# Linear attention and channel mix on one core: fused passes for the first batch, and another written-out order

## The chip, the cores and the metric

The kernel runs on one core of one Trainium2 chip. The metric is the device time of one execution in microseconds (us). The core has five engines with an instruction queue each: TensorE (PE, the matrix products), VectorE (DVE), ScalarE (ACT), GpSimd (POOL, which here mostly issues loads) and SyncE (SP, which issues stores and small copies). An engine takes its queue in order; an instruction that waits holds up all that stand behind it. Transfers are made by 16 DMA engines, whichever queue issued them.

## What is computed

Eight batches b, eight heads, 576 tokens s, 64 dimensions per head; F = 1024. All inputs and the output are fp32, the kernel computes in bf16 with fp32 sums.

```python
kv  = einsum('bhsd,bhse->bhde', k, v)
u   = einsum('bhsd,bhde->bhse', q, kv)
x   = u / sqrt(mean(u*u, -1) + 1e-6) * g_norm        # per head; then heads side by side: 512 channels
xp  = x one token later, zero in front
xk  = mu_k*x + (1-mu_k)*xp ;  xr = mu_r*x + (1-mu_r)*xp
out = sigmoid(xr @ w_r) * (relu(xk @ w_k)**2 @ w_v)
```

## The kernel before

The work is cut into named *pieces*, each a handful of instructions for one engine. A string, ORDER, lists all pieces by name, and `Plan.emit` issues them in that order; so every engine's queue has its pieces in the order of that one list. A name may end in `@A` or `@D`, which puts the piece on ACT or DVE. `z:512` is a matmul on zeros that computes nothing and stands where PE would have no work.

**Attention, batch b.** Channels are held in two halves z = 0, 1 (four heads each). Batches 0 and 1 go half by half, with names such as `kv0.1` (batch 0, z = 1); from batch 2 on both halves go together (`kv4.01`). The pieces of one batch, in the order in which each needs the one before:

- `ld.k`, `ld.v`, `ld.q` load from HBM, on POOL (L221, L226), with a cast to bf16. The first half of k and v of batch 0 comes over SP as fp32 (`ldh`, L236) and is cast by `cst`. `ld.wk`, `ld.wv`, `ld.wr` load the weights (L252). Each of k, v and q has three buffers, so a load for a later batch waits until a buffer is free. POOL also waits, at each load, for the load eight places before it.
- `kv` (PE, L265) makes the 64 x 64 products, `kc` copies them out of PSUM, `ks` (PE, L271) sorts even and odd rows apart, `kd` copies again. `tq` (DVE, L349) transposes q.
- `u` (PE, L282) gives u, 128 channels x 288 tokens at a time for each of two channel blocks, transposed, into a PSUM tile `ps`. There are four such tiles in all.
- `uc` multiplies u by g_norm and writes it to SBUF as `uT` (DVE L136 or ACT L134). `sq` (ACT, L370) writes the squares; `ss` (PE, L395 in batches 0 and 1, L379 later) sums them over each head's 64 channels; `rs` (ACT, L288) makes 1/rms. From batch 2 on 1/rms is made once per head and `sp` (SP, L417) spreads it over the channels by eight small DMAs per batch.
- `mul` (DVE, L392) makes x = uT times 1/rms, into `xT`. `d` (L300) is x minus the token before. `mk` and `mr` scale d by mu - 1 (DVE L136 or ACT L134) into `md`, and `xk`, `xr` (L313) add x.

**Channel mix, group g of 512 tokens** (nine groups; group g needs the batches that its tokens lie in: group 0 batch 0, group 1 batches 0 and 1, group 2 batches 1 and 2, and so on): `k` (PE, L469 in group 0, L494 later), `relu` (ACT, L452), `ksq` (DVE, L480, L509), `v` (PE, L541), `r` (PE, L521), `sig` (ACT, L531), `out` (DVE, L554), `st` (SP, L443). In group 1 the k pieces are halved again (`k1.4.0`, `k1.4.1`).

In ORDER, mix pieces of earlier groups stand between the attention pieces of later batches, so that PE has matmuls while a batch's chain runs over DVE and ACT.

Of the kernel before, what the change touches and what calls it, by code (L numbers as in the profile page):

```python
# [10 lines left out]
ALU = mybir.AluOpType  # L11
# [1 line left out]


ORDER = """
ldh.k ldh.v ld.q0.0 small table seta setp ident ld.v0.1 ld.k0.1 ld.q0.1 ld.q1.0 ld.v1.0 ld.k1.0 perm ld.wk0 ld.wk1 ld.k1.1 ld.v1.1 ld.wv0 ld.q1.1 ld.wv1 ld.wr ld.k2.01 ld.v2.01 ld.q2.01 zz cst.k0@A cst.k1@A cst.v1@D cst.v0@A z:512 z:512 z:512 z:512 z:512 z:512 z:512 z:512 z:512 z:512 z:512 z:512 z:512 z:512 z:512 z:512 kv0.0 setb tq0.0.1 kc0.0@A z:512 z:512 ks0.0 tq0.0.0 tr9 kd0.0@D z:512 z:512 z:512 u0.0.1 sq0.01 kv0.1 ld.v3.01 ld.k3.01 cols u0.0.0 sq0.00 uc0.01@D uc0.00@A kc0.1@D z:512 z:512 z:512 ss0.00 rs0.00 z:512 ss0.01 tq0.1.0 tq0.1.1 ld.q3.01 mul0.00 ks0.1 kd0.1@A d0.00 rs0.01 z:512 z:512 u0.1.0 uc0.10@A sq0.10 u0.1.1 uc0.11@A z:512 z:512 z:512 z:512 z:512 ss0.10 mul0.01 d0.01 mk0.00@D kv1.0 sq0.11 xk0.00 rs0.10 ss0.11 rs0.11 tq1.0.1 kc1.0@D ks1.0 tq1.0.0 kd1.0@A z:512 z:512 u1.0.0 mk0.01@D u1.0.1 sq1.00 xk0.01 k0.100 uc1.00@A uc1.01@A k0.000 sq1.01 mul0.10 d0.10 mk0.10@D xk0.10 mul0.11 d0.11 k0.010 mr0.11@A mk0.11@D xk0.11 k0.011 relu0.01 ss1.1 rs1.1 mr0.10@D xr0.10 k0.001 k0.101 relu0.00 mr0.00@D relu0.10 kv1.1 k0.110 ss1.0 ksq0.00 ksq0.10 k0.111 kc1.1@A v0.3.0 tq1.1.0 v0.2.0 tq1.1.1 ld.q4.01 ld.k4.01 ld.v4.01 rs1.0 relu0.11 ks1.1 kd1.1@D ksq0.11 mr0.01@A xr0.11 ksq0.01 xr0.00 v0.1.0 mul1.0 d1.0 u1.1.1 uc1.11@A u1.1.0 sq1.10 sq1.11 v0.0.0 xr0.01 v0.0.1 uc1.10@A v0.1.1 ss1.3 rs1.3 ss1.2 v0.3.1 rs1.2 mk1.0@D xk1.0 r0.0 mul1.1 d1.1 r0.1 sig0.0 r0.2 r0.3 sig0.1 v0.2.1 kv2.01 ld.v5.01 ld.k5.01 mk1.1@D xk1.1 out0.0 k1.2.0 k1.0.0 k1.1.0 out0.1 kc2.01@D ks2.01 tq2.01.1 tq2.01.0 k1.3.0 k1.2.1 k1.3.1 mr1.0@A kd2.01@A relu1.1 k1.0.1 u2.01.1 sq2.11 mr1.1@D k1.1.1 relu1.0 k1.6.0 k1.7.0 uc2.01@D uc2.11@D sq2.01 ksq1.1 u2.01.0 k1.6.1 k1.7.1 sq2.10 xr1.1 uc2.10@D k1.4.0 sq2.00 k1.5.0 uc2.00@D ss2 rs2 sp2.0 kv3.01 ld.v6.01 ld.q5.01 k1.4.1 k1.5.1 xr1.0 relu1.2 r1.0 kc3.01@D ksq1.0 ks3.01 kd3.01@A relu1.3 tq3.01.1 tq3.01.0 ld.q6.01 ld.k6.01 ksq1.2 r1.1 v1.0.0 ksq1.3 u3.01.0 uc3.10@D sig1.0 sq3.10 v1.1.0 v1.0.1 tq4.01.1 v1.1.1 uc3.00@D u3.01.1 tq4.01.0 sq3.00 uc3.11@A r1.2 r1.3 out1.0 sq3.11 v1.2.0 v1.3.0 sq3.01 ss3 mul2.0 sig1.1 kv4.01 ld.k7.01 ld.q7.01 ld.v7.01 sp2.1 rs3 kc4.01@A d2.0 v1.3.1 mk2.0@D xk2.0 st0.0 ks4.01 kd4.01@A v1.2.1 st0.3 uc3.01@A st0.2 mul2.1 d2.1 mk2.1@D xk2.1 u4.01.0 sq4.10 st0.1 uc4.10@A k2.2 uc4.00@A sq4.00 out1.1 st1.0 mr2.0@D k2.3 k2.0 k2.1 relu2.0 ksq2.0 relu2.1 ksq2.1 k2.4 k2.5 relu2.2 k2.6 k2.7 sp3.0 relu2.3 xr2.0 v2.3.0 mr2.1@D kv5.01 mul3.0 ksq2.2 u4.01.1 sq4.11 ksq2.3 sp3.1 d3.0 v2.2.0 st1.1 v2.2.1 uc4.11@A v2.1.0 uc4.01@A mul3.1 sq4.01 mr3.0@D ss4 xr3.0 kc5.01@A v2.1.1 v2.3.1 rs4 sp4.1 xr2.1 sp4.0 r2.2 v2.0.0 d3.1 mk3.1@A mr3.1@D xr3.1 xk3.1 tq5.01.0 ks5.01 kd5.01@A mk3.0@D xk3.0 v2.0.1 r2.3 sig2.1 out2.1 st2.3 r2.0 tq6.01.1 r2.1 sig2.0 out2.0 k3.2 k3.3 relu3.1 ksq3.1 k3.0 tq5.01.1 k3.4 k3.5 relu3.2 k3.1 mul4.1 d4.1 mr4.1@D relu3.0 ksq3.0 k3.6 k3.7 ksq3.2 u5.01.0 st2.0 st1.3 uc5.10@D relu3.3 ksq3.3 v3.3.0 uc5.00@A xr4.1 r3.0 mul4.0 sq5.10 tq6.01.0 r3.1 sq5.00 mk4.1@D sig3.0 r3.2 d4.0 mk4.0@D xk4.0 st2.1 r3.3 sig3.1 v3.3.1 kv6.01 kc6.01@A u5.01.1 uc5.11@D uc5.01@A sq5.11 tq7.01.1 v3.2.0 v3.2.1 ks6.01 kd6.01@D out3.1 v3.0.0 v3.0.1 st2.2 sq5.01 u6.01.1 xk4.1 ss5 rs5 sp5.0 v3.1.0 v3.1.1 mr4.0@D xr4.0 uc6.11@A st1.2 sq6.11 sq6.01 uc6.01@A tq7.01.0 k4.4 k4.5 k4.2 out3.0 st3.0 u6.01.0 relu4.2 uc6.10@D uc6.00@D sq6.10 k4.3 relu4.1 sq6.00 k4.0 k4.1 relu4.0 ksq4.1 k4.6 kv7.01 ss6 st3.2 ksq4.0 k4.7 r4.0 r4.1 kc7.01@D mul5.0 d5.0 relu4.3 ksq4.3 v4.1.0 sp5.1 mul5.1 rs6 st3.1 d5.1 ks7.01 kd7.01@D sp6.1 v4.2.0 ksq4.2 v4.3.0 sig4.0 u7.01.0 uc7.10@D v4.0.0 v4.2.1 v4.0.1 mk5.0@D mr5.1@A uc7.00@A sq7.00 r4.2 sq7.10 r4.3 mk5.1@D xk5.1 xr5.1 mr5.0@A sig4.1 mul6.1 xr5.0 xk5.0 d6.1 mk6.1@A sp6.0 mul6.0 v4.3.1 v4.1.1 out4.0 out4.1 st4.0 st4.2 k5.6 k5.7 relu5.3 ksq5.3 k5.2 k5.3 relu5.1 st4.3 ksq5.1 k5.0 k5.1 relu5.0 u7.01.1 sq7.01 sq7.11 d6.0 xk6.1 mk6.0@D uc7.11@D mr6.0@D k5.4 k5.5 st3.3 ksq5.0 r5.2 xr6.0 r5.3 st4.1 mr6.1@D ss7 uc7.01@A relu5.2 rs7 v5.1.0 sig5.1 ksq5.2 r5.0 sp7.0 r5.1 sig5.0 v5.0.0 v5.0.1 v5.1.1 xk6.0 k6.0 k6.1 relu6.0 xr6.1 r6.0 sp7.1 out5.0 st5.0 st5.1 v5.3.0 mul7.1 v5.2.0 k6.4 k6.5 relu6.2 ksq6.2 d7.1 ksq6.0 k6.2 k6.3 relu6.1 r6.1 mul7.0 r6.2 sig6.0 r6.3 k6.6 k6.7 v5.2.1 ksq6.1 v6.2.0 v6.3.0 d7.0 relu6.3 v6.1.0 mr7.0@A mk7.0@D xk7.0 v6.0.0 sig6.1 mr7.1@A mk7.1@D xk7.1 k7.4 k7.5 xr7.0 ksq6.3 v6.1.1 v6.0.1 out6.0 v6.3.1 v6.2.1 out6.1 st6.3 k8.2 k8.3 relu8.1 k7.2 v5.3.1 out5.1 k7.6 k7.7 k8.0 relu7.3 k7.3 relu7.1 ksq8.1 relu7.2 st6.0 st6.1 ksq7.3 st6.2 xr7.1 k7.0 k7.1 r7.0 relu7.0 r7.2 r7.1 r7.3 k8.1 k8.6 sig7.0 ksq7.2 ksq7.0 ksq7.1 k8.7 relu8.3 st5.3 relu8.0 r8.2 r8.3 st5.2 ksq8.0 v7.3.0 ksq8.3 v7.3.1 v7.1.0 v7.1.1 sig8.1 k8.4 k8.5 relu8.2 ksq8.2 v7.0.0 v7.0.1 v7.2.0 v7.2.1 sig7.1 out7.1 st7.2 st7.3 out7.0 v8.1.00 r8.0 r8.1 v8.2.00 v8.2.10 st7.0 v8.0.00 out8.20 sig8.0 st7.1 v8.1.10 st8.20 out8.10 v8.0.10 st8.10 v8.3.00 v8.3.10 out8.00 st8.00 out8.30 v8.3.01 v8.3.11 st8.30 out8.31 st8.31
"""


# [37 lines left out]
def kernel(  # L57
# [13 lines left out]
    nc = tc.nc  # L71
# [18 lines left out]
    X0 = 2  # L90
# [203 lines left out]
    def blends(b, z, name, x0, w, deps, mds, dd):  # L294
        xT = xTs[(NZ * b + z) % NX]
        cur, prev = slice(X0 + x0, X0 + x0 + w), slice(X0 - 1 + x0, X0 - 1 + x0 + w)
        cs, r0 = slice(x0, x0 + w), S * (b % RB) + x0

        def diff(_):
            nc.vector.tensor_tensor(out=get(dd)[:, :, cs], in0=xT[:, :, cur], in1=xT[:, :, prev], op=ALU.subtract)  # L300

        df = add("d" + name, "D", diff, deps=deps, bufs=[dd, x_buf[(b, z)]])
        done = {}
        for key, dst, m0 in (("k", xk, 0), ("r", xr, NHP)):
            md = mds[key]

            def mul(eng, md=md, m0=m0):
                for y in range(2):
                    hp = m0 + 2 * z + y
                    scale(eng, get(md)[:, y, cs], dd.t[:, y, cs], cols[:, hp:hp + 1])  # L310

            def plus(_, md=md, dst=dst):
                nc.vector.tensor_tensor(out=dst[:, 2 * z:2 * z + 2, r0:r0 + w], in0=md.t[:, :, cs], in1=xT[:, :, cur],  # L313
                                        op=ALU.add)

            m = add(f"m{key}" + name, "DA", mul, deps=[df, p_cols], bufs=[dd, md])
            done[key] = add(f"x{key}" + name, "D", plus, deps=[m] + x_free.get((b - RB, key), []),
                            bufs=[md, x_buf[(b, z)]])
        return done
# [3 lines left out]
    def attention(b):  # L323
# [40 lines left out]
        for z in range(NZ):  # L364
            for i, (c0, c1) in enumerate(PARTS):
                name, ps, w, cs = f"{b}.{z}{i}", us[z][i], c1 - c0, slice(c0, c1)
                uT, sq = bufs[z]["uT"], bufs[z]["sq"]
                uc = add("uc" + name, "DA", lambda eng, ps=ps, uT=uT, cs=cs, w=w: scale(
                    eng, get(uT)[:, :, cs], ps.t[:, :, 0:w], cols[:, 8:9]), deps=[pu[(z, i)], p_cols], bufs=[ps, uT])
                sq_ = add("sq" + name, "A", lambda _, ps=ps, sq=sq, cs=cs, w=w: nc.scalar.activation(  # L370
                    out=get(sq)[:, :, cs], in_=ps.t[:, :, 0:w], func=AF.Square), deps=[pu[(z, i)]], bufs=[ps, sq])
# [15 lines left out]
        for z in range(NZ):  # L387
            uT, sq, rs, dd = (bufs[z][t] for t in ("uT", "sq", "rs", "d"))
            xT, xb = xTs[(NZ * b + z) % NX], x_buf[(b, z)]

            def mul(_, cs, uT=uT, rs=rs, xT=xT):
                nc.vector.tensor_mul(out=xT[:, :, X0 + cs.start:X0 + cs.stop], in0=uT.t[:, :, cs], in1=rs.t[:, :, cs])  # L392

# [3 lines left out]
            if b == 0:  # L397
                muls = []
                for i, (c0, c1) in enumerate(PARTS):
                    ps, w, cs = Buf("ps"), c1 - c0, slice(c0, c1)  # L400
                    s = add(f"ss{b}.{z}{i}", "T", lambda _, ps=ps, c0=c0, w=w, sq=sq: [ones_mm(_, ps, y, c0, w, y, sq)
                            for y in range(2)], deps=[secs[(z, i)][1], p_setb], bufs=[ps, sq])
                    p = add(f"rs{b}.{z}{i}", "A", lambda _, ps=ps, w=w, cs=cs, rs=rs: rms(_, get(rs)[:, :, cs], ps.t[:, :, 0:w]),
                            deps=[s], bufs=[ps, rs])
                    muls = muls + [add(f"mul{b}.{z}{i}", "D", lambda _, cs=cs, mul=mul: mul(_, cs),
                                       deps=[p, secs[(z, i)][0], p_setb], bufs=[uT, rs, xb])]
                    done = blends(b, z, f"{b}.{z}{i}", c0, w, muls, mds[z], dd)
                    for key in "kr":
                        x_ready[b][key].append(done[key])
# [200 lines left out]
```

## Time and profile before

| | |
|---|---|
| median of 3 runs | 200.04 us (199.97 to 200.71) |
| the profiled execution | 200.29 us |
| its span, first to last instruction | 198.5 us |
| PE busy | 189.4 us, 95% of the span |
| DVE busy | 136.1 us, 69% |
| ACT busy | 123.6 us, 62% |
| DMA | 30.63 MB, mean 154 GB/s |

A page of the profile gives busy time by engine, the span in 40 slices, the chain of work that ended last, and groups of like instructions by source line. Beside it the trace can be asked for the instructions of an engine in order of time: start, duration, engine, line, operation, out<-in, how many, and in brackets how long the engine sat idle before and what released it. Busy time of one engine is an average over stretches with different limits; what decides is which wait ends last in a stretch.

### The profile page before, as it was taken

Reading aid. Unit: us, or ns where it says so; the run is one execution under the profiler, and the core shown is the slowest. Engines: PE = TensorE matmul, PEld = TensorE weight load, DVE = VectorE, ACT = ScalarE, POOL = GpSimd, SP = SyncE. Lnnn points to the kernel's source line nnn. Section 1 sums busy time; section 2 is a strip of 40 time slices with the busy share of each in tenths; the row PEclk is TensorE's granted clock in tenths of the full one; section 3 lists DMA queues with packets and bytes.
Section 4 is the critical chain, followed back from the end, with each engine's and each line's share of the span. In section 5 each row is a group of like instructions: output and inputs, shape, how many; then the busy total and the mean of one; then the engine's idle time right before and its main releaser. Section 6 shows DMA issues by size and latency. Waiting matters only on the chain.

```text
span 198.5 us, 4247 instructions
## 1 busy us (share of the span) xinstructions
PE 189.4 (95%) x1741; PEld 94.1 (47%) x1765; DVE 136.1 (69%) x242; ACT 123.6 (62%) x161; POOL 23.8 (12%) x42
## 2 busy tenths in 40 slices
PE   7998999998997999999999999999999999999992
PEld 2444864443544454444547744434444444444451
DVE  1579939999899378999986679896348246410631
ACT  3378995769897776848676697689255423652120
POOL 7843332220412100000000000000000000000000
PEclk9999999999999999999999999999999999999999
DMA  6999999999999999999706523242500017000064
GB/s 218 217 207 210 193 204 212 211 207 214 207 237 273 272 239 243 217 241 262 187 0 188 147 47 77 95 169 58 170 0 2 0 45 273 2 0 0 28 239 159
DMA packets 21031, 30.63 MB, mean 154 GB/s; under 512 B 1932, under 2 KB 14484, under 8 KB 21012
## 3 DMA queue, kind: packets, MB, share of 16 engines
q0 software_dynamic: 11280, 16.19, 45.6%
q1 hardware_dynamic: 9588, 14.03, 22.4%
q8 instruction: 14, 0.23, 0.5%
q10 hardware_dynamic: 144, 0.13, 0.2%
q14 instruction: 5, 0.04, 0.1%
HBM read 33.56 MB, written 9.44 MB: 217 GB/s over the span
## 4 chain that ended last, share of the span: by engine, by line
PE 66%; DMA 27%; POOL 3%; issue 1%; DVE 0%; POOLq 0%
PE ps L541 25%; PE ps L494 25%; DMA v<-in_v_dram 13%; PE ps L521 12%; DMA k<-in_k_dram 9%; DMA w_k<-in_moe_w_k_dram 6%; PE ps L282 2%; PE ps L265 1%; POOL k L226 1%; PE ps L379 1%; POOL v L226 1%; POOL q L221 1%; POOL perm L189 1%; PE ps L271 0%; DVE out L568 0%
## 5 line engine op out<-in xcount | busy, mean ns | idle before, releaser
L541 PE MATMUL ps<-w_v,sqk 128*128 128x512 bf16 (+1 forms) x287 | 66.4, 373 | 0.9 <-issue 0.5
L494 PE MATMUL ps<-xk,w_k 128*128 128x512 bf16 (+1 forms) x280 | 58.1, 355 | 0.6 <-issue 0.3
L452 ACT ACTIVATE relu<-ps 128x1024 bf16<-128x1024 f32 x36 | 36.1, 1025 | 35.6 <-PE ps L494 33.7
L541 PEld LDWEIGHTS <-sqk 128*128 128x128 bf16 x296 | 27.8, 98 | 32.1 <-issue 2.0
L494 PEld LDWEIGHTS <-w_k 128*128 128x128 bf16 x288 | 27.5, 98 | 27.3 <-issue 1.6
L509 DVE TENSOR_TENSOR sqk<-relu 128x1024 bf16<-128x1024 bf16 x32 | 21.7, 687 | 22.8 <-ACT relu L452 22.8
L521 PE MATMUL ps<-w_r,xr 128*128 128x512 bf16 x140 | 33.5, 379 | 0.3
L554 DVE TENSOR_TENSOR out<-ps,sig 128x1024 f32<-128x1024 f32 x16 | 19.2, 1218 | 12.4 <-PE ps L541 8.5
L531 ACT ACTIVATE sig<-ps 128x1024 bf16<-128x1024 f32 x18 | 18.3, 1022 | 9.2 <-PE ps L521 9.1
L370 ACT ACTIVATE sq<-ps 128x576 bf16<-128x576 f32 x32 | 20.0, 652 | 5.7 <-PE ps L282 4.1
L521 PEld LDWEIGHTS <-xr 128*128 128x128 bf16 x144 | 14.0, 98 | 16.5 <-issue 0.2
L136 DVE TENSOR_SCALAR md<-d,cols 128x576 bf16<-128x576 bf16 (+1 forms) x54 | 16.4, 347 | 0.3
L349 DVE STREAM_TRANSPOSE qT<-q 128x576 f32<-128x576 f32 (+1 forms) x20 | 14.9, 762 | 2.3 <-DMA q<-in_q_dram 2.1
L134 ACT ACTIVATE uT<-ps,cols 128x576 bf16<-128x576 f32 x19 | 13.7, 741 | 2.0 <-PE ps L282 1.9
L392 DVE TENSOR_TENSOR xT<-uT,rs 128x1152 bf16<-128x1152 bf16 (+1 forms) x18 | 12.4, 686 | 2.4 <-DMA rs<-rsc 2.3
L134 ACT ACTIVATE md<-d,cols 128x576 bf16<-128x576 bf16 (+1 forms) x18 | 12.0, 714 | 2.7 <-DVE d L300 2.7
L136 DVE TENSOR_SCALAR uT<-ps,cols 128x576 bf16<-128x576 f32 x13 | 10.4, 813 | 4.7 <-PE ps L282 3.2
L144 ACT ACT_TABLE_LOAD x10 | 12.8, 1283 | 0.9 <-PEq L594 0.7
L313 DVE TENSOR_TENSOR xr<-md,xT 128x1152 bf16<-128x1152 bf16 (+1 forms) x18 | 12.3, 687 | 0.7 <-ACT md L134 0.6
L313 DVE TENSOR_TENSOR xk<-md,xT 128x1152 bf16<-128x1152 bf16 (+1 forms) x18 | 12.4, 691 | 0.5
L300 DVE TENSOR_TENSOR d<-xT 128x1152 bf16<-128x1152 bf16 (+1 forms) x18 | 12.4, 691 | 0.4
L437 PE MATMUL ps<-zero 128*128 128x512 bf16 x32 | 10.8, 478 | 1.7 <-DVE ident L167 1.2
(49 smaller groups left out, 110.8 us busy)
## 6 DMA issues: line engine op xcount, KB each, us to landing
out_dram<-out SPq DMA_DIRECT2D x35, 256.0 KB, 3.1
k<-in_k_dram POOLq DMA_DIRECT2D x6, 576.0 KB, 24.8
v<-in_v_dram POOLq DMA_DIRECT2D x6, 576.0 KB, 25.4
q<-in_q_dram POOLq DMA_DIRECT2D x6, 576.0 KB, 25.1
rs<-rsc SPq DMA_DIRECT2D x48, 72.0 KB, 5.4
q<-in_q_dram POOLq DMA_DIRECT2D x4, 288.0 KB, 8.8
w_k<-in_moe_w_k_dram POOLq DMA_DIRECT2D x2, 512.0 KB, 12.5
w_v<-in_moe_w_v_dram POOLq DMA_DIRECT2D x2, 512.0 KB, 16.3
```

Source lines behind the costliest of these rows:

```text
L134: nc.scalar.mul(out=dst, in_=src, mul=col)
L136: nc.vector.tensor_scalar(out=dst, in0=src, scalar1=col, scalar2=None, op0=ALU.mult)
L313: nc.vector.tensor_tensor(out=dst[:, 2 * z:2 * z + 2, r0:r0 + w], in0=md.t[:, :, cs], in1=xT[:, :, cur], op=ALU.add)
L349: nc.vector.transpose(out=dst[part, js], in_=src[part, js])
L370: sq_ = add("sq" + name, "A", lambda _, ps=ps, sq=sq, cs=cs, w=w: nc.scalar.activation(out=get(sq)[:, :, cs], in_=ps.t[:, :, 0:w], func=AF ...
L452: nc.scalar.activation(out=get(rt), in_=ps.t, func=AF.Relu)
L494: nc.tensor.matmul(get(ps)[:, fc % 2, a0:a1], w_k_sb[:, cc, 128 * fc:128 * fc + 128], xk[:, cc, x0:x0 + a1 - a0], start=(cc == 0), stop=(c ...
L509: nc.vector.tensor_mul(out=get(sqk)[:, 2 * f2:2 * f2 + 2, :], in0=rt.t, in1=rt.t)
L521: nc.tensor.matmul(get(ps)[:, ci % 2, :], xr[:, cc, n0:n0 + 128], w_r_sb[:, cc, :], start=(cc == 0), stop=(cc == NHP - 1))
L531: nc.scalar.activation(out=get(sg), in_=ps.t, func=AF.Sigmoid)
L541: nc.tensor.matmul(get(ps)[:, bank, cs], sqk.t[:, fc, 128 * ci:128 * ci + 128], w_v_sb[:, fc, cs], start=(fc == 0), stop=(fc == NFC - 1))
L554: dv = add(f"out{g}.{c2}", "D", lambda _, ps=ps, sg=sg, ot=ot: nc.vector.tensor_mul(out=get(ot), in0=ps.t, in1=sg.t), deps=ms + [sg_done], ...
```

## The change

In batch 0 only, `uc` goes. `mul` there takes u straight out of PSUM and multiplies by g_norm and by 1/rms in one DVE instruction. `mk` and `xk`, and `mr` and `xr`, become one pass on DVE per channel block, `(d * (mu-1)) + x`, two instructions of 288 tokens for a piece. u's PSUM tile is therefore held until `mul`. No other batch's instructions change.

And ORDER is another one: 33 matmuls on zeros in place of 34; `uc` and the batch 0 scalings gone; loads, attention pieces, mix pieces, their engines (`@A`, `@D`) and stores placed anew.

```diff
@@ blends
+            if b == 0:
+                def both(_, m0=m0, dst=dst):
+                    for y in range(2):
+                        hp = m0 + 2 * z + y
+                        nc.vector.scalar_tensor_tensor(out=dst[:, 2 * z + y, r0:r0 + w], in0=dd.t[:, y, cs], scalar=cols[:, hp:hp + 1],
+                                                       in1=xT[:, y, cur], op0=ALU.mult, op1=ALU.add)
+
+                done[key] = add(f"x{key}" + name, "D", both, deps=[df, p_cols], bufs=[dd, x_buf[(b, z)]])
+                continue
@@ attention
-                uc = add("uc" + name, "DA", lambda eng, ps=ps, uT=uT, cs=cs, w=w: scale(
+                uc = None if b == 0 else add("uc" + name, "DA", lambda eng, ps=ps, uT=uT, cs=cs, w=w: scale(
...
+            def mul_ps(_, cs, ps, rs=rs, xT=xT):
+                nc.vector.scalar_tensor_tensor(out=xT[:, :, X0 + cs.start:X0 + cs.stop], in0=ps.t[:, :, 0:cs.stop - cs.start],
+                                               scalar=cols[:, 8:9], in1=rs.t[:, :, cs], op0=ALU.mult, op1=ALU.mult)
...
-                    muls = muls + [add(f"mul{b}.{z}{i}", "D", lambda _, cs=cs, mul=mul: mul(_, cs),
-                                       deps=[p, secs[(z, i)][0], p_setb], bufs=[uT, rs, xb])]
+                    muls = muls + [add(f"mul{b}.{z}{i}", "D", lambda _, cs=cs, mul=mul_ps, pu_=us[z][i]: mul(_, cs, pu_),
+                                       deps=[p, pu[(z, i)], p_cols, p_setb], bufs=[us[z][i], rs, xb])]
```

Of the two orders, the loads in POOL's queue, first to last:

```
before  q0.0 v0.1 k0.1 q0.1 q1.0 v1.0 k1.0 wk0 wk1 k1.1 v1.1 wv0 q1.1 wv1 wr k2 v2 q2 v3 k3 q3 q4 k4 v4 v5 k5 v6 q5 q6 k6 k7 q7 v7
after   q0.0 q0.1 k0.1 v0.1 v1.1 wk0 k1.1 wk1 q1.1 k1.0 v1.0 q1.0 wv0 wv1 wr v2 q2 k2 q3 v3 k3 v6 v5 v4 k5 q4 k4 v7 k6 q5 q6 k7 q7
```

PE's pieces from the end of the first zeros to the first matmul of mix 0 (z: a matmul on zeros):

```
before  kv0.0 z z ks0.0 tr9 z z z u0.0.1 kv0.1 u0.0.0 z z z ss0.00 z ss0.01 ks0.1 z z u0.1.0 u0.1.1 z z z z z ss0.10 kv1.0 ss0.11 ks1.0 z z u1.0.0 u1.0.1 k0.100
after   kv0.0 tr9 ks0.0 z z u0.0.0 z z z ss0.00 u0.0.1 z z z z ss0.01 kv0.1 z z ks0.1 z z u0.1.0 u0.1.1 z z ss0.10 z z k0.000
```

PE's pieces from kv3 to kv5:

```
before  kv3.01 k1.4.1 k1.5.1 r1.0 ks3.01 r1.1 v1.0.0 u3.01.0 v1.1.0 v1.0.1 v1.1.1 u3.01.1 r1.2 r1.3 v1.2.0 v1.3.0 ss3 kv4.01 v1.3.1 ks4.01 v1.2.1 u4.01.0 k2.2 k2.3 k2.0 k2.1 k2.4 k2.5 k2.6 k2.7 v2.3.0 kv5.01
after   kv3.01 v1.1.1 ks3.01 r1.0 r1.1 u3.01.0 v1.0.1 r1.2 r1.3 u3.01.1 v1.3.0 v1.2.0 v1.2.1 ss3 v1.3.1 kv5.01 k2.0 k2.2 k2.3 k2.1 k2.6 k2.7 k2.4 k2.5 ks5.01 kv4.01
```

DVE's pieces of batch 0's half 0 and 1 after the change: `tq0.0.0 kc0.0 tq0.0.1 cols tq0.1.0 mul0.00 d0.00 tq0.1.1 mul0.01 d0.01 xk0.01 xk0.00 mul0.10 d0.10 xk0.10 mul0.11 d0.11 xk0.11`; and from mix 1's end on `out1.1 tq4.01.1 ksq2.1 ksq2.0 mul3.0 tq4.01.0 ksq2.3 kc4.01`. SP's queue: before `sp2.0 sp2.1 st0.0 st0.3 st0.2 st0.1 st1.0 sp3.0 sp3.1 st1.1 sp4.1`, after `sp2.1 sp2.0 st0.2 st0.0 st0.1 sp3.0 sp3.1 st1.0 st1.1 st0.3 sp4.0`.

## Prediction

> **What bounds the kernel now.** I read the page first, then TensorE's timeline, then the timeline of POOL (which issues the loads) with each load's time to landing, and last the chain of waits.
>
> ```profile
> span 198.5 us, 4247 instructions
> ...
> PE   7998999998997999999999999999999999999992
> ...
> DMA  6999999999999999999706523242500017000064
> ```
>
> Each digit is a tenth of a slice of 198.5/40 = 4.96 us. PE is full nearly throughout; the DMA engines are full from slice 2 to slice 19, up to 94 us. So there are two bounds at once: PE's work, and the stream of inputs. They meet where PE asks for a load. The PE timeline names the one place after 31 us where PE idles for a load:
>
> ```profile
> 49.47 0.77 PE L265 MATMUL ps<-v,k 64*64 64x64 bf16 x72
> ...
> 61.02 0.43 PE L379 MATMUL ps<-sq,heads 128*32 128x288 bf16 x8
> 62.30 0.77 PE L265 MATMUL ps<-v,k 64*64 64x64 bf16 x72 [0.85 <-DMA v<-in_v_dram]
> ```
>
> L265 is a kv piece. The one at 62.30 is kv4.01; it stood ready at 61.45 and waited 0.85 us for v4. The chain that ended last runs through the same load, and from there PE alone is on it:
>
> ```profile
> 37.22 24.95 DMA v<-in_v_dram
> 62.17 0.14 issue
> 62.30 0.77 PE ps L265 x72
> ...
> 188.62 6.08 PE ps L541 x36
> ```
>
> PE's other idle stretches after 62.3 are "issue" gaps of 0.16 us and less. So from 62.30 to PE's end at 194.72 the kernel is 132.4 us of packed PE work, and any wait of PE after that moves the end one for one.
>
> **When loads land.** POOL's issue times plus each one's time to landing, loads numbered in the order of issue: 15th (w_r) 33.9, k2 36.9, v2 39.6, 18th q2 42.4, v3 45.2, k3 48.5, 21st q3 51.4, q4 54.2, k4 57.7, 24th v4 62.2, 25th v5 67.7, 26th 72.3, 27th 76.5, 28th 79.3, 29th 82.1, 30th 86.0, 31st 89.8, 32nd 93.2, 33rd 98.8. All land in order. Undisturbed, a whole-batch load takes (51.4 - 33.9)/6 = 2.9 us. After 50 us the SP queue's transfers share the engines. In 54 to 70 us the loads moved 2.03 MB and the SP queue 2.08 MB; at 0.59 MB in 2.9 us the loads alone would have moved 3.25 MB, so the SP queue's 2.08 MB cost 1.22 MB of loads, 6.0 us, or 2.9 us per MB. One batch's eight rs<-rsc pieces (0.59 MB) then cost 1.7 us, one store (0.26 MB) 0.75 us. Check on today's 25th: 51.4 + 4 x 2.9 + 1.7 + 5 stores x 0.75 = 68.5 against 67.7 measured.
>
> The Trainium skill ("DMA: Bandwidth & Descriptors", section on queues, rings and completion order) says that each DMA engine takes turns between the queue rows that have work, packet by packet. The rows agree in kind: spacing 5.5 us from v4 to v5, nearly twice 2.9.
>
> **The change, part by part.** It has two halves, fusing in batch 0 and a new order.
>
> *Fusing.* In batch 0, four uc pieces go (one on DVE at 0.82 us, three on ACT at 0.73), and the four muls at 0.46 now read PSUM. No row shows that fused form. From below it costs what mul cost, 0.46; from above uc and mul in series, 0.82 + 0.46 = 1.28. I take 0.82: one pass over 576 fp32 out of PSUM, which is L136's row. The eight blends lose two scalings each (0.245 per half, or 0.48 on ACT) and a sum (0.46), and get two fused passes of 288. From below each is 0.245 (the scaling alone), from above 0.46 (a whole sum). I take 0.46, next start after 0.38 as in the rows of sums. Sum on DVE: before 4 x 0.46 + 0.82 + 6 scalings x 0.49 + 8 x 0.46 = 9.3; after 4 x 0.82 + 16 x 0.38 = 9.4. So DVE gains nothing; ACT gives up 3 x 0.73 + 2 x 0.96 = 4.1 us. With 0.245 per pass DVE would gain 2.2.
>
> The Trainium skill ("VectorE: DVE Perf Modes", rules for kernel authors) speaks against this half: chained Vector operations should not be fused for speed. The rows above, summed, say the same of DVE and not of ACT.
>
> *Opening, by rows.* u0.0.0 starts about 10.35 (10.19 now; kc0.0 stands behind a transpose of 0.68 on DVE). Then sq 0.65, ss 0.41, rs 0.74 with hand-overs of 0.05: mul0.00 at 12.8 (now 14.14). Then 0.82 + d 0.46 + tq0.1.1 0.70 gives 14.7; mul0.01 0.82, d 0.46, four fused passes 3 x 0.38 + 0.46: xk0.00 at 17.6. The first matmul of mix 0 comes at 17.7 instead of 19.66. But at 19.66 PE had also done kv1.0 0.69, ks1.0 0.33, u1.0 0.69 and ss0.11 0.25, together 1.96, which now come later. So the opening is worth 17.7 + 1.96 - 19.66 = 0. With the fused pass at 0.245 it is 0.5 better; with the form out of PSUM at 1.28 it is 2 x 0.46 = 0.9 worse. All of this stands ahead of the load waits below: a faster opening only makes PE wait longer there.
>
> *Loads.* The first 15 are the same ones in another order, so w_r, the last of them, lands at 33.9 as now. Then come v2, q2, k2, q3, v3, k3 (18th 42.4, 21st 51.4), and now **v6 as 22nd, then v5, v4, k5, q4, k4, v7, k6**. v6 is needed only by kv6; it takes a slot ahead of v5, v4 and k5. kv5 is also moved ahead of kv4 on PE, and all of mix 2's k pieces stand behind kv5.
>
> I now put PE's arrival at each kv, from its time before plus the pieces now ahead of it, against the load that it needs.
> - kv2 needs the 18th, 42.4. Before 40.38; now eight k1 halves (0.43) more and one v piece (0.86) less: 43.0. No wait.
> - kv3 needs the 21st, 51.4. Before 49.31; two k1 halves and two v pieces more: 51.9. No wait, without margin.
> - kv5 takes the place of kv4. PE is done with what stands ahead at 61.45 + v1.2.1 and v1.3.1 (2 x 0.86) = 63.2. It needs k5, the 25th: 51.4 + 4 x 2.9 + one rs group 1.7 + three stores 2.2 = 66.9. (v4's buffer comes free with kv3, at about 52; k5 is behind v4 in POOL's queue. Two loads are then still on their way, so the stream doesn't run dry.) **PE waits 3.7 us.** Everything behind kv5 in PE's queue waits too: k2.0 to k2.7, which need no load.
> - kv4 needs k4, the 27th: 51.4 + 6 x 2.9 + two rs groups 3.4 + about three stores 2.2 = 74.4. PE arrives at 66.9 + 0.7 + 32 matmuls x 0.216 + ks5 0.2 = 74.7. No wait to 1 us.
> - kv6 needs k6, the 29th, 82.1 by today's row; PE arrives at 74.7 + 0.7 + 7 v pieces 6.0 + ks4, u4 1.0 = 82.4. kv7 comes beyond 100 for a load at 93.2.
>
> Sum: kv5 at 67.0 against what is now 62.30 + 1.73 = 64.0, so PE's end moves 3.0 us, 194.7 to 197.7; the tail of 3.8 us is unchanged. The 0.85 of today is within this, since 64.0 counts it. The profiled execution was 200.29 us (span 198.5 and 1.8 around it); 203.3 by it. The median of the runs shown, 200.04, is 0.25 lower: **203.0**.
>
> **Bounds.** Loads at the fastest spacing (2.7, q2 behind v2) and one store fewer put k5 at 65.4, 1.5 sooner: 201.5. k4 in today's 27th slot, 76.5, puts kv4 1.8 later: 204.8. Behind kv4 a wait is added on DVE: mul3.0 waits for sp3's pieces, and tq4.01.0, ksq2.3 and kc4.01 are queued behind it, for whom ks4.01 and u4 wait on PE. ss3 is done about 63, rs3 about 64.5; four pieces take 4.0 us on SP and 5.4 to 8.3 to land: 73.9 to 76.8. The early end costs nothing, the late one about 1.5 us; I take nothing, as the median of the landings is the early end.
>
> **Rivals.**
> 1. *The loads are no later than PE* (faster). If k5 came at 51.4 + 4 x 2.7 = 62.2 and k4 at 67.6, as if rs and stores took nothing, neither kv5 nor kv4 would wait; today's 0.85 goes, and perhaps 0.5 of the opening: 198.9. It decides where k5 lands before 63.2. Against it: v4 to v5 took 5.5 us. For it: fewer stores stand ahead.
> 2. *Partly so* (no change): k5 at 64 to 64.8, stores late enough to pass behind it: 200.0 to 200.8.
> 3. *The opening fails*: DVE, which has to read PSUM later, holds four PSUM tiles longer and delays the k pieces. Since PE has 3.7 us in hand at kv5, it has to lose more than that to show. Then 205 and more, with waits for DVE ahead of 50 us.
> 4. *Loads at half pace while the SP queue has work.* From 52 to 65 us SP would be busy 13 us, which costs 6.5 in place of 3.9: k5 at 69.5, 205.6. For it: 5.5 us from v4 to v5; against it: 3.6 us each from q3 to v4, with SP busy from 50.5. This is what the skill's turn-taking makes of it if every packet counts alike.
>
> **How the numbers follow.** Forecast (wait at kv5, or split between kv5 and kv4, 201.3 to 205.0) 0.72; rival 1 0.07; rival 2 0.10; rivals 3 and 4 0.11. A measurement of this kernel can tell about 0.5% from no change, here 199.04 to 201.04. Faster 0.07, same 0.11, slower 0.82. The range leaves out rival 1, half of rival 2 and the far end of 3 and 4: 200.6 to 205.3.
>
> **What would show it.** PE's row of L265 x72 near 67 with idle before it of 2.5 to 4 us, released by DMA k. k3 landing near 51.4 and k5 at 65 to 68. The first k0 matmul at 17 to 18.5. PE packed from kv4 on. Fused passes of 0.35 to 0.46, the one out of PSUM near 0.82. I am wrong if kv5 starts by 64 without a wait, or if the order has waits for DVE or ACT above 1 us behind kv4, which I only laid out as far as kv6.

## The result, and the profile after

The changed kernel takes 207.88 us (median of 6 runs, 207.15 to 213.71), the kernel before in the same sessions 200.47 (6 runs, 199.97 to 200.75). One run of the six, 213.71, stands apart with a mean granted clock of 0.95 against 0.98 and is left out of the ratio. The ratio is 1.036, with an interval of 1.034 to 1.039. The forecast was 203.0, in 200.6 to 205.3: the direction was right, the time lies above the range, and the forecast loss was less than half of the measured one. The profiled execution took 208.0 us, with a span of 206.2 against 198.5: 7.7 us to explain.

The page of the changed kernel, the lines that answer to those shown of before, and with them the granted clock:

```profile
span 206.2 us, 4250 instructions
...
PE   7998899999994599999999999999999999999992
...
PEclk9999999999999579999999999999999999999999
DMA  6999999999999999996304425204400202601044
```

A slice is now 206.2/40 = 5.16 us; counted from 0, most of the loss is in slices 12 and 13, from 62 to 72 us, where PE is 0.4 and 0.5 busy. The granted clock falls there too, to 0.5 and 0.7 in slices 13 and 14. After 77 us both lines are full to the end, as they were before.

PE's timeline of the changed kernel over that place (L265 is a kv piece, L507 k, L554 v, L388 ss):

```profile
62.90 0.43 PE L388 MATMUL ps<-sq,heads 128*32 128x288 bf16 x8
63.26 1.04 PE L554 MATMUL ps<-w_v,sqk 128*128 128x512 bf16 x4
67.90 1.18 PE L265 MATMUL ps<-v,k 64*64 64x64 bf16 x72 [3.60 <-ACT rsc L288]
70.61 8.92 PE L507 MATMUL ps<-xk,w_k 128*128 128x512 bf16 x32 [1.53 <-DVE xk L313]
79.36 0.39 PE L271 MATMUL ps<-kvn,perm 128*128 128x128 bf16 x4
79.68 0.78 PE L265 MATMUL ps<-v,k 64*64 64x64 bf16 x72
```

The row of 67.90 is kv5. It starts 0.9 us later than the forecast said (67.0), after the idle time that it said (3.60 against 3.7), but what released it is ACT's rsc, not a load. Then there is a second wait, 1.53 us for xk, which the forecast did not have. Then mix 2's 32 k matmuls take 8.92 us, where 32 x 0.216 = 6.9 was expected. The clock explains the last. PE's windows of the changed kernel (length, PE busy and its instructions, granted clock, DMA share, GB/s):

```profile
64.00:65.00 1.00, 0.30 (x2) 1.00 1.14 247
65.00:66.00 1.00, 0.00 (x0) 1.00 1.03 228
66.00:67.00 1.00, 0.00 (x0) 1.00 1.00 236
67.00:68.00 1.00, 0.10 (x9) 0.77 1.11 270
68.00:69.00 1.00, 1.00 (x72) 0.50 1.12 277
...
73.00:74.00 1.00, 1.00 (x4) 0.50 1.18 215
74.00:75.00 1.00, 1.00 (x5) 0.82 1.18 217
```

PE falls idle at 64.30. The clock is halved at about 67.5 (0.77 is 0.54 of that window at 1.0 and the rest at 0.5) and is back at about 74.4 (0.82 is 0.36 of the window at 0.5): it is half through kv5 and the first 3.8 us of k2.

The chain of waits of the changed kernel says where xk came from (rsc is 1/rms before its spread; L430 is SP's spread of it over the partitions, L405 mul, L300 d, L136 md, L313 xk):

```profile
51.52 1.28 ACT L144
...
52.82 0.74 ACT rsc L288
...
59.07 7.78 DMA rs<-rsc
...
66.97 0.77 DVE xT L405
...
69.21 1.35 DVE xk L313 x2
70.56 0.05 issue
70.61 8.92 PE ps L507 x32
```

Read from the bottom: k2 waits for xk2, xk2 for mul2, mul2 for the last piece of batch 2's spread (SP sends eight one after the other, and the last lands at 66.85), and the spread for rs2 on ACT at 52.82, right behind its table load. Before, the same steps stood here, on ACT and then on DVE:

```profile
49.70 0.74 ACT L288 ACTIVATE rsc<-ps,eps 128x576 bf16<-128x576 f32 x1
```

```profile
61.52 0.76 DVE L392 TENSOR_TENSOR xT<-uT,rs 128x1152 bf16<-128x1152 bf16 x1
...
63.80 0.76 DVE L313 TENSOR_TENSOR xk<-md,xT 128x1152 bf16<-128x1152 bf16 x1
```

So rs2 is 3.1 us later than before and the end of xk2 6.0 us later (64.56 to 70.55). Before, xk2 was ready 0.9 us ahead of k2's start at 65.45: there was no room for it.

**The sum**, from the two profiled executions. When PE is done with what stands ahead of kv5, it is 64.30; before, the same work and no more was done at 61.45 + 1.73 = 63.18: 1.1 us are lost by then. The two idle stretches are 3.60 + 1.53, against 0.85 before: 4.3. At half clock k2 takes 8.92 in place of 7.07 and kv5 1.18 in place of 0.78 (rows at full clock: k2's from the second experiment below, a kv piece's at 79.68 above): 2.25. Together 7.65 of 7.7.

### The profile page after: what moved, and what is told of

The parts are those of the page before. It is cut to its first block, busy times and chain, and to the rows that moved or that the text cites. A ratio compares the mean times of both kernels' runs of the same rounds, so it can differ in the third digit from the quotient of the medians.

```text
span 206.2 us, 4250 instructions
## 1 busy us (share of the span) xinstructions
PE 194.0 (94%) x1764; PEld 94.9 (46%) x1764; DVE 136.4 (66%) x231; ACT 122.7 (59%) x160; POOL 23.9 (12%) x42
## 4 chain that ended last, share of the span: by engine, by line
PE 75%; DMA 10%; ACT 3%; DVE 3%; POOL 3%; SPq 2%; issue 1%; POOLq 0%; DVEq 0%; ACTq 0%
PE ps L554 27%; PE ps L507 26%; PE ps L534 13%; DMA w_k<-in_moe_w_k_dram 7%; DMA rs<-rsc 4%; PE ps L482 3%; SPq L430 2%; PE ps L282 2%; PE ps L265 2%; ACT relu L465 1%; PE ps L271 1%; ACT sq L379 1%; PE ps L388 1%; DVE xk L313 1%; ACT L144 1%
## 5 line engine op out<-in xcount | busy, mean ns | idle before, releaser
L554 PE MATMUL ps<-w_v,sqk 128*128 128x512 bf16 (+1 forms) x296 | 67.2, 374 | 0.2 <-ACT relu L465 0.2
L507 PE MATMUL ps<-xk,w_k 128*128 128x512 bf16 (+1 forms) x288 | 59.9, 363 | 1.5 <-DVE xk L313 1.5
L554 PEld LDWEIGHTS <-sqk 128*128 128x128 bf16 x296 | 27.8, 98 | 32.3 <-issue 2.6
L507 PEld LDWEIGHTS <-w_k 128*128 128x128 bf16 x288 | 28.1, 99 | 30.2 <-issue 3.4
L134 ACT ACTIVATE md<-d,cols 128x576 bf16<-128x576 bf16 x20 | 14.4, 769 | 6.5 <-DVE d L300 6.5
L405 DVE TENSOR_TENSOR xT<-uT,rs 128x1152 bf16<-128x1152 bf16 x14 | 10.4, 751 | 9.2 <-DMA rs<-rsc 9.1
L300 DVE TENSOR_TENSOR d<-xT 128x1152 bf16<-128x1152 bf16 (+1 forms) x18 | 12.4, 691 | 0.5
L136 DVE TENSOR_SCALAR uT<-ps,cols 128x576 bf16<-128x576 f32 x13 | 10.4, 811 | 3.0 <-PE ps L282 2.6
L136 DVE TENSOR_SCALAR md<-d,cols 128x576 bf16<-128x576 bf16 x36 | 11.5, 364 | 0.3
L134 ACT ACTIVATE uT<-ps,cols 128x576 bf16<-128x576 f32 x15 | 10.9, 743 | 1.0 <-PE ps L282 1.0
L265 PE MATMUL ps<-v,k 64*64 64x64 bf16 x576 | 8.1, 200 | 3.6 <-ACT rsc L288 3.6
L226 POOL DMA_DIRECT2D v<-in_v_dram x9 | 6.6, 739 | 38.8 <-PE ps L265 33.2
## 6 DMA issues: line engine op xcount, KB each, us to landing
q<-in_q_dram POOLq DMA_DIRECT2D x4, 288.0 KB, 10.2
```

The source lines that it names most:

```text
L134: nc.scalar.mul(out=dst, in_=src, mul=col)
L136: nc.vector.tensor_scalar(out=dst, in0=src, scalar1=col, scalar2=None, op0=ALU.mult)
L507: nc.tensor.matmul(get(ps)[:, fc % 2, a0:a1], w_k_sb[:, cc, 128 * fc:128 * fc + 128], xk[:, cc, x0:x0 + a1 - a0], start=(cc == 0), stop=(c ...
L554: nc.tensor.matmul(get(ps)[:, bank, cs], sqk.t[:, fc, 128 * ci:128 * ci + 128], w_v_sb[:, fc, cs], start=(fc == 0), stop=(fc == NFC - 1))
```

## The experiments

The theory that came to stand, D in the later expectations: batch 2's spread is late, and holds PE twice. rsc has a single buffer, so rs3 on ACT can't write it while the spread of batch 2 still reads it; until rs3 has read ss3's PSUM tile, none of the four PSUM tiles is free for kv5. And xk2 holds k2. PE has no other work left, since the new order has all of mix 1 behind it and k2 in front. The idle time then halves the clock. The rival from the forecast: k5's load, which lands at 67.4 here (forecast 66.9), holds kv5 and everything else follows.

**1. k5 loaded early.** In POOL's queue, k5 and v6 change places:

```diff
-... v3 k3 v6 v5 v4 k5 q4 k4 ...
+... v3 k3 k5 v5 v4 v6 q4 k4 ...
```

> The changed kernel with one swap in POOL's queue: ld.k5.01 where ld.v6.01 stands (22nd), ld.v6.01 where ld.k5.01 stands (25th). Theory A (two waits in series, and a clock that falls after them): kv5 no longer waits for k5 and starts at about 64.3, but k2.0 still waits for xk2, whose last sum ends at 70.5 because batch 2's spread of 1/rms lands at 66.9; PE stands idle 65.0 to 70.6, the clock falls as before, and the time moves by less than 0.7 us: 207.2 to 208.2. Rival B (the late load k5 is the whole of the loss): the 3.6 us wait at kv5 goes with nothing in its place, 203.5 to 204.5, or 201.5 to 202.5 if the clock then stays up too.

Median 207.45 us (207.06, 207.84, 208.19, and one run of 203.69). k5 landed at 53.7, 13.7 us sooner than in the changed kernel, and kv5 moved by one. PE's timeline:

```profile
66.91 0.77 PE L265 MATMUL ps<-v,k 64*64 64x64 bf16 x72 [2.89 <-ACT rsc L288]
69.62 0.61 PE L507 MATMUL ps<-xk,w_k 128*128 128x512 bf16 x1 [1.93 <-DVE xk L313]
```

These rows are of the run of 208.19. In it the load is not what holds kv5 by itself. The run of 203.69 has a mean granted clock of 1.00, in a span of 201.9, and lies where the rival expected it. It is one run, and no profile shows its waits. The half clock costs k2 about 2.9 us in the profiled run (69.62 to 79.58 in place of 7.07), so the kept clock could be most of the 4.5 us between the two, and the rest is open.

**2. Zeros in the idle time.** Matmuls on zeros into the tiles that kv5 and k2 then overwrite; the output is the same:

```diff
-... v1.3.1 mr2.1@A kv5.01 ... xk2.0 k2.0 ...
+... v1.3.1 mr2.1@A [16 matmuls on zeros] kv5.01 ... xk2.0 [7 matmuls on zeros] k2.0 ...
```

> The changed kernel with matmuls on zeros in PE's queue where it stood idle: 16 ahead of kv5.01 (3.5 us at full clock, into kv5's own PSUM tile) and 7 ahead of k2.0 (1.5 us, into that one's tile). They compute nothing and wait for nothing new. Theory A: the granted clock, 0.50 from 67.9 to about 74.5 in the changed kernel, stays at 1.0; kv5 still starts about 67.9 and k2.0 about 70.7, but k2's 32 matmuls take 6.9 us in place of 8.9, and the end comes 2.0 us sooner: 205.9 (205.5 to 206.3). If the slow matmuls have another cause than the idle PE (contention, the load stream), the clock stays at 0.50 and the time at 207.9 or above.

208.78 us, ratio 1.042 (1.039 to 1.045): a miss on the time, and telling. PE's timeline:

```profile
67.03 3.61 PE L599 MATMUL ps<-zero 128*128 128x512 bf16 x16 [2.43 <-ACT rsc L288]
70.57 0.90 PE L265 MATMUL ps<-v,k 64*64 64x64 bf16 x72
...
72.92 7.07 PE L511 MATMUL ps<-xk,w_k 128*128 128x512 bf16 x32
```

The zeros need no load and no data, only kv5's PSUM tile; they waited until 67.03 for the same ACT rsc. So the wait is for the tile. They then stood ahead of kv5 and cost what they were to save. But the granted clock was 1.00 throughout, and k2 took 7.07 us for 8.92: the half clock costs 1.85 us on k2 alone.

**3. Fusing alone, in the order of before.** The new batch 0 code with the old ORDER, without uc, mk0 and mr0. In the old order kv0.1 and others would ask for PSUM tiles that are now held until mul, so kv0.1, kv1.0, u1.0 and some neighbours had to move behind mul0:

```diff
-... u0.0.1 sq0.01 kv0.1 ... mul0.00 ks0.1 ... ss0.10 mul0.01 ... kv1.0 ... u1.0.0 u1.0.1 k0.100 k0.000
+... u0.0.1 sq0.01 ... mul0.00 kv0.1 ks0.1 ... mul0.01 ... ss0.10 ss0.11 kv1.0 ... k0.000 u1.0.0 u1.0.1 k0.100
```

> The fused passes alone: the order of before, with uc, mk and mr of batch 0 left out, and in the opening kv0.1 moved behind mul0.00, kv1.0 behind ss0.11 and u1.0 behind mul0.10 and mul0.11, since u's PSUM tiles are held until mul. Loads and all from kv2 on stand as before. Theory A: the loss lies in the order from kv2 on, so this is within 0.7 us of the kernel before, 199.8 to 201.0, with the wait for v4 at 62.3 still there. Rival C (the fused passes or the held tiles cost the time): 203 or more, with kv4 later than 64.

214.53 us (209.96 to 218.37): a miss, and inconclusive on fusing. In the profiled execution, 215.12 us, the opening became 7.6 us longer (kv2 at 48.02 for 40.38), with PE waiting for ACT and DVE in batch 0 and the granted clock at 0.50 from 15.9 to 19.3 and from 22.7 to 26.2. A wait of 4.96 us for a PSUM tile follows at 80.27. That is the price of my own order as much as of the code. What it shows is that the fused form does not fit into the old opening with these moves.

**4. The new order, not fused.** uc, mk0 and mr0 put back into batch 0:

```diff
-... u0.0.0 sq0.00 ... mul0.00 d0.00 ... xk0.01 ...
+... u0.0.0 sq0.00 uc0.00@D ... mul0.00 d0.00 ... mk0.01@D xk0.01 ...
```

> The order of after alone: batch 0 as in the kernel before, with uc ahead of rs (two on DVE, two on ACT), mk on DVE ahead of each xk, mr on ACT for two parts and on DVE for two. Theory A: PE reaches kv5 up to a few us later, but has 3.6 us in hand there, so the time is that of after within 0.7 us: 207.3 to 208.6. Rival C (the fused passes cost the time): 204 or less.

209.67 us, ratio 1.048 (1.045 to 1.050): 1.8 us above the changed kernel, and a miss, since the same time was expected within 0.7 us. SP's spread of batch 2 starts at 55.07 here, against 53.59, and kv5 at 69.44 after 3.65 us of idle. So fusing is worth some 1.8 us in this order, and a delay of the opening comes out at the end in full, since the late chain begins on PE and moves with it.

**5. A second buffer for rsc.**

```diff
-"rsc": (1,
+"rsc": (2,
```

> The changed kernel with two buffers in place of one for rsc, the tile that rs writes from batch 2 on and that the spread (sp) reads. Theory D, formed on the first four runs: kv5 waits for a PSUM tile, the one that ss3 wrote; that is freed by rs3 on ACT; rs3 waits until sp2's eight small DMAs have read the single rsc, to 66.9; and xk2, which needs what sp2 brings, holds k2.0 to 70.6. With two buffers rs3 runs at about 63.1 and kv5 starts when k5 has landed, 65 to 67.4; k2.0 still starts at about 70.6, since xk2 is as late as before. Time 207.9 within 1 us. If the single buffer alone were the cause, 203.5 to 205.

206.97 us, ratio 1.033 (1.029 to 1.038), 0.9 under the changed kernel, with intervals that overlap. PE's timeline:

```profile
66.73 1.18 PE L265 MATMUL ps<-v,k 64*64 64x64 bf16 x72 [2.55 <-DMA k<-in_k_dram]
69.28 8.98 PE L507 MATMUL ps<-xk,w_k 128*128 128x512 bf16 x32 [1.37 <-DVE xk L313]
```

rs3 no longer waits, and what appears is the forecast's own wait: kv5 for k5, which landed at 66.7. In the changed kernel the two ended within 0.5 us of each other. Behind kv5 stands xk2, as before. It came 1.3 us sooner than in the changed kernel, not at the 70.6 that was expected: the spread started at 53.46, within 0.2 us of the changed kernel's, and landed sooner. k2 takes 8.98 us, again at half clock.

**6. Batch 2's spread asked for sooner.** rs2's table is loaded ahead (behind sig0.1, left out below), ss2 and rs2 go ahead of a v piece and a relu, and v1.1.1 behind r1.1:

```diff
-... sq2.10 sq2.00 ... relu1.3 uc2.00@D v1.1.0 v1.0.0 ss2 rs2 mr1.0@D sp2.1 sp2.0 ... v1.1.1 xr1.0 ks3.01 kd3.01@A r1.0 r1.1 ...
+... uc2.00@D sq2.10 sq2.00 ss2 rs2 sp2.1 sp2.0 relu1.3 v1.1.0 v1.0.0 mr1.0@D ... xr1.0 ks3.01 kd3.01@A r1.0 r1.1 v1.1.1 ...
```

> The changed kernel with sp2 started about 2 us sooner and nothing else: the ACT table for rs is loaded behind sig0.1, where ACT was idle 0.8 us, ss2 stands ahead of v1.1.0, relu1.3 behind rs2, v1.1.1 behind r1.1. Theory D: rs2 ends about 51.7 in place of 53.6, the spread has landed by about 65, kv5 starts at 65.3 to 66.5, k2.0 at 68.7; the time falls by 1.5 to 2.5 us, to 205.4 to 206.4, and by up to 2 more if the shorter wait leaves the clock up. If the load of k5 sets kv5 (rival B), kv5 stays at 67.4 and beyond, and the time at 207.5 or above.

204.22 us, ratio 1.021 (1.016 to 1.026), 3.7 under the changed kernel. But the profiled execution is the longest of the four, 206.36 against 204.04 to 204.24, and in it the reason expected is not to be seen: the spread starts at 53.69, no sooner. kv2 was 0.8 us late there, and the edit had put the last uc2 ahead of the last sq2, so that ACT waited 0.94 us for DVE. What moved is PE's work: kv5 comes at 66.86 with no wait, then 1.38 us for xk2 and later 1.64 for a PSUM tile. No idle time in this stretch was over 1.7 us, the clock stayed at 1.00, and the halves of k2 took 3.63 and 3.61 us. It agrees with the clock's part of D and leaves the spread's start untested: when it came in the three shorter runs, no profile shows.

**7. kv2 ahead of mix 1's k.** kv2 and half of u2 ahead of most k1 halves, k2 loaded ahead of v2 and q2:

```diff
-... ld.v2 ld.q2 ld.k2 ... k1.4.0 k1.5.0 xk1.1 out0.0 k1.4.1 k1.5.1 tq2.01.1 k1.2.0 k1.3.0 k1.2.1 ... k1.3.1 relu1.1 kv2.01
+... ld.k2 ld.v2 ld.q2 ... k1.4.0 k1.5.0 xk1.1 out0.0 kv2.01 ld.v5 kc2.01@A k1.4.1 k1.5.1 tq2.01.1 ks2.01 k1.2.0 k1.3.0
```

> The changed kernel with batch 2's attention ahead of most of mix 1's k pieces again: kv2.01 behind k1.5.0, u2.01.1 ahead of k1.3.1, and k2 loaded ahead of v2 and q2 (positions 16 to 18). Theory D: the chain kv2, u2, ss2, rs2, sp2, xk2 starts 2 to 3 us sooner, sp2 at about 51 in place of 53.6, k2.0 at 67.5 to 68.5 in place of 70.6: 205 to 206, and down to 203 if the clock stays up. Rival B (loads): kv5 waits for k5 all the same, 207 or more.

209.11 us, ratio 1.043 (1.036 to 1.049): a miss. Two runs took 207.55 and 207.99, two 210.23 and 210.27; the last is the profiled one. In it kv2 came at 41.55, 2.3 us sooner, but the other half of u2 at 49.3, then a relu and the table load, and rs2 at 53.84, later than before the edit. kv2 alone does not set the spread; the last of u2, sq2 and ss2, and what ACT has queued ahead of rs2, do.

**8. Splice.** The changed kernel up to the end of mix 0, fused passes and all; then, from kv2 on, the old order of pieces, and of loads from the 16th on:

```diff
-... sig0.1 k1.4.0 k1.5.0 xk1.1 out0.0 k1.4.1 ...         [the new order to the end]
+... sig0.1 ld.q4 ld.k4 ld.v4 v0.2.1 kv2.01 ld.v5 ld.k5 xk1.1 out0.0 k1.2.0 ...   [the order of before to the end]
```

> The changed kernel up to the end of mix 0 (fused passes and the new opening in it), and from kv2 on the order of before, with the loads from the 16th on in before's order too. Theory D: what costs the time lies from kv2 on. PE comes to kv2 about 0.9 later than in the kernel before, kv4's wait of 0.85 for v4 takes that up, the spreads are in time: 200.2 (199.7 to 201.2). If the fused passes or the new opening cost it, 203 or more.

200.64 us, ratio 1.001 (0.999 to 1.004): the time of before. PE's timeline:

```profile
61.64 0.43 PE L388 MATMUL ps<-sq,heads 128*32 128x288 bf16 x8
62.72 0.77 PE L265 MATMUL ps<-v,k 64*64 64x64 bf16 x72 [0.66 <-DMA v<-in_v_dram]
...
65.86 7.08 PE L507 MATMUL ps<-xk,w_k 128*128 128x512 bf16 x32
```

The fused code and the new opening cost nothing that shows at the end; the loss is in the order from kv2 on, that of the loads included. SP starts the spread at 51.08 here, k2 follows at 65.86 without a wait.

**9. Both of kv5's waits taken away.** The edits of 1 and 5 together.

> The changed kernel with both of kv5's waits taken away at once: rsc gets a second buffer (so rs3 need not wait for batch 2's spread) and k5 is loaded in the place of v6 (landing near 54). Theory D (batch 2's spread is late and holds kv5 by its buffer and k2 by xk2): kv5 starts at 64 to 65 without a wait over 1 us, but the first k2 matmul still starts at 69 to 70.5, behind xk2, now with an idle stretch of 3 to 5 us just ahead of it; the clock falls as before and the time stays at 206 to 207.5. Rival (kv5's own two waits are the whole loss, xk2 only follows from them): k2 starts by 66.5, and the time is 203 to 204.5.

208.01 us, ratio 1.041 (1.037 to 1.044). kv5 starts at 64.48, straight behind its predecessor. PE's timeline:

```profile
63.51 1.04 PE L554 MATMUL ps<-w_v,sqk 128*128 128x512 bf16 x4
64.48 0.78 PE L265 MATMUL ps<-v,k 64*64 64x64 bf16 x72
70.55 0.61 PE L507 MATMUL ps<-xk,w_k 128*128 128x512 bf16 x1 [5.29 <-DVE xk L313]
```

k2 starts within 0.1 us of where the changed kernel starts it: kv5 won 3.4 us, and all of it went into the wait for xk2. This is the plainest evidence for D: load and rsc buffer stand ahead of a later bound, and taking both away buys nothing. (The time is no better than with one of them taken away; the longer single idle stretch again halves the clock. What makes xk2 late is read from the chain of waits above; no run moved it alone.)

**10. The splice with its two waits filled.** The second half of w_k loaded ahead of k1.1, and the v pieces v1.2.1 and v1.3.1 ahead of kv4, as in the changed kernel:

```diff
-... ld.k1.1 ld.wk1 ... sig1.1 kv4.01 ... v1.3.1 ... v1.2.1 ...
+... ld.wk1 ld.k1.1 ... sig1.1 v1.3.1 v1.2.1 kv4.01 ...
```

> The splice (the changed kernel's opening and fused batch 0, the order of before from kv2 on) with its two remaining waits of PE filled: the second half of w_k is loaded ahead of k1.1 (0.52 us of wait at 20.9 in the splice), and the v pieces v1.3.1 and v1.2.1 stand ahead of kv4 (0.66 us of wait for v4 at 62.7). Theory D: both waits go, nothing else moves, and the time is 199.3 to 199.9, 0.3 to 0.6% under the kernel before. Rival (what is won ahead of kv4 is lost behind it, at k2, whose xk2 comes no sooner): 200.2 to 200.8, with a wait for DVE ahead of k2.

204.34 us, ratio 1.019 (1.016 to 1.022): a miss on both sides of the expectation. PE's timeline:

```profile
21.02 0.76 PE L265 MATMUL ps<-v,k 64*64 64x64 bf16 x36 [1.37 <-DMA k<-in_k_dram]
...
64.60 0.78 PE L265 MATMUL ps<-v,k 64*64 64x64 bf16 x72
66.01 0.38 PE L271 MATMUL ps<-kvn,perm 128*128 128x128 bf16 x4 [0.63 <-ACT kvn L128]
66.86 0.32 PE L282 MATMUL ps<-qT,kv 32*64 32x288 bf16 x4 [0.46 <-ACT kv L128]
68.21 0.64 PE L282 MATMUL ps<-qT,kv 32*64 32x288 bf16 x12 [1.03 <-DVE out L567]
```

The wait for w_k became one of 1.4 us for k1.1. And the wait for v4 went, but v1.3.1 and v1.2.1 had another task where they stood, between kv4 and ks4 and between ks4 and u4: they covered ACT's two casts of kv4 (0.63 and 0.46) and the freeing of PSUM tiles (1.03). With these gaps, none over 1.03 us, the granted clock fell to 0.50 from 68.3 to 71.7. So filling 0.66 us of wait with work that already covered something cost 2.1 us of waits and about 1.5 of clock. The profiled execution took 205.0 at a mean clock of 0.987; three others took 203.3 to 203.7 at 0.996 to 1.00, so the clock's part is not paid in every run.

None of the ten is faster than the kernel before; the splice equals it.

## Why the prediction was right in direction and too small

- **Fusing's own terms nearly held.** The form out of PSUM took 0.82, as forecast. A fused pass took 0.51, above the 0.46 that was called the upper bound, and four in a row 1.81, so the next starts after 0.43 and not 0.38: the sum on DVE is about 10.2 us, not 9.4. The first k0 matmul still came at 16.99 against 17.7, since u0.0.0 started 0.7 us sooner than forecast (9.67).
- **"So the opening is worth 0"** was 1.1 us off by 64 us: kv2 at 43.89 (forecast 43.0), kv3 at 52.40 (51.9), PE free at 64.30 (63.2). The changed kernel's PE waits 1.12 us at 21.23 for the second half of w_k, which the new load order puts behind k1.1; I had not set that load against its user.
- **"A faster opening only makes PE wait longer there"** is wrong here. It holds if the wait ends with a load. This one ends with a chain that begins on PE. Experiment 4 delays the opening and the end goes along.
- **"PE waits 3.7 us" at kv5**: 3.60. The load was a real bound (k5 at 67.4; it is what remains in experiment 5). But the tile behind rsc, which I did not look at, ended 0.5 us later. That the number was right is luck: a second cause ended close to the first.
- **The step that failed** is the one behind it: "k2.0 to k2.7, which need no load", and then kv4's arrival at "66.9 + 0.7 + 32 matmuls x 0.216". I followed loads, and took k2 as ready as soon as kv5 was through. k2 needs xk2, and xk2 the spread of batch 2. I worked out the same chain for batch 3 ("a wait is added on DVE: mul3.0 waits for sp3's pieces") and never for batch 2, although my own shift of kv2 by 2.6 us moved its start. "Waits for DVE or ACT above 1 us behind kv4" were what I said would prove me wrong; the one that came stood ahead of kv4. It costs 1.53 us of wait, and experiment 9 shows it to be the last of the bounds.
- **The second term that failed** is 0.216 us for each matmul after an idle stretch. An idle stretch of 3.6 us here did not cost 3.6 but 3.6 and the half clock behind it, 2.25 us. Experiment 2 takes this apart: the same wait for the tile, clock kept, k2 in 7.07.
- **Rivals.** The first two needed k5 by 64.8; it landed at 67.4. (The 198.9 of the first counts from the profiled 200.29; from the median, as the forecast does, it is 198.7.) The third, on the opening, came to 1.1 us of its 205 and more, and by another mechanism (a load, not PSUM tiles). The fourth, loads at half pace, is refuted: k5 landed at 67.4, not 69.5.

What stays open: how much would be won if the spread alone started 3 us sooner with nothing else moved (6 and 7 both failed to bring that about); and why its last piece took 7.78 us to land, against 5.8 to 5.9 for the pieces of before. This adds 1.9 us or more to the 3.1 of its start, and I did not separate it from the loads and stores around it. Another 0.5 of the 6.0 us is DVE's order: both xk2 sums now stand behind the last mul2, 3.58 us from its start to their end against 3.04.

## What to carry to other kernels

When a new order moves a stage, follow its whole chain over all engines to the next work that PE asks for, for every batch from the first one moved, and not the loads alone; and count buffers with a single copy as part of that chain. Take away one wait in a packed place and look at what is ready next: in this kernel three bounds lay within 3.2 us (67.4, 67.85, 70.55), and removing the first two bought nothing. A piece of work that is independent of its neighbours may be the cover of a hand-over, so before it is moved, say what it covers.

## What the runs showed of the hardware

PE's granted clock was the surprise. It was halved 3.2 us after PE fell idle in the changed kernel, 4.7 us after in experiment 9, and only 2.1 and 2.2 us after in experiments 5 and 7: there is no fixed delay. But how long it stayed half is regular. It was half for 6.82 us in the changed kernel and in experiments 1, 4 and 5, for 3.42 in 9 and 10, and for 10.24 in 7: two, one and three times 3.41 us. Its ends can be worked out from rows such as these, of experiments 9 and 7:

```profile
69.00:70.00 1.00, 0.00 (x0) 0.97 1.12 287
...
73.00:74.00 1.00, 1.00 (x5) 0.82 1.20 244
```

```profile
67.00:68.00 1.00, 0.00 (x0) 0.67 1.12 255
...
77.00:78.00 1.00, 1.00 (x5) 0.71 1.12 207
```

In experiment 3, where the clock fell three times, at 15.92, 22.74 and 77.36, the falls lie 2 and 16 times 3.41 us apart. So these rows look like a clock that is judged once in 3.41 us, on a grid that does not start with the idle time. With the grid laid through all eight profiles that show a fall, PE was busy for 1.7 us or less in each stretch that ended with a fall, and for 2.2 or more in every other one at full clock; for 2.6 or more in each that ended with a return, and for 2.3 or less in every other one at half clock. What a gap costs then depends on where it falls on the grid as well as on its length.

The Trainium skill ("TensorE: Matmul & The Clock Gate", Part 1 on the clock gate) says that the clock goes to half after an idle window of about 3.4 us and back after about as long of sustained work, and that this window runs freely. The 3.42, 6.82 and 10.24 us agree with a free window of that length; a window need not be wholly idle, as experiment 10 shows. No gap there was over 1.03 us, but PE was busy for only 1.28 of the 3.41 us up to 68.31, and the clock still fell to 0.50. Experiment 6, with gaps of 1.38 and 1.64 us that had 3.6 us of work between them, kept it at 1.00, and so did 2.43 us of idle followed by zeros in experiment 2. So a gap of 2.4 us need not cost more than itself, and three of 0.46 to 1.03 us in a row did.
